# Late mask rows for the odd head, nine unread products and a buffer for expert 0's input, in a fused attention, router, expert and gated-layer kernel

## The chip, the cores and the metric

One core of one Trainium2 chip runs the whole program in one launch. The metric is device time in microseconds (us), the median of the runs shown; lower is better. In the profile PE is the matrix engine, PEld its weight loads, DVE the vector engine, ACT the scalar engine, POOL the GpSimd engine and SP the engine that issues most DMAs (SPq in a row is its queue).

## The reference

Three stages, each feeding the next. Attention has 2 batches of 8 heads, 768 positions and 64 columns; a query sees only the keys whose nearest centroid (of 16) is its own:

```python
q_assign = np.argmax(np.einsum('bhsd,hcd->bhsc', q_n, c_n), axis=-1)
k_assign = np.argmax(np.einsum('bhsd,hcd->bhsc', k_n, c_n), axis=-1)
mask = q_assign[:, :, :, None] == k_assign[:, :, None, :]
scores = np.where(mask, scale * np.matmul(q, k.transpose(0, 1, 3, 2)), -1000000000.0)
...
return np.matmul(attn, v).astype(np.float32)
```

A router then sends each of the 1536 rows to one of 8 experts by the largest of 8 logits (at most 384 rows each); an expert computes `relu(x @ w1) @ w2` with 512 x 1024 and 1024 x 512 weights, scaled by the gate. A gated layer with 512 x 1536 weights ends it: `(silu(x @ w_gate) * (x @ w_val)) @ w_out`.

## The kernel before

Numbers are kept as a rounded high part and a low part of the rest (H and L, or W1h and W1l), and products are added from three pairings, so that single-pass matmuls give nearly full precision.

**Attention.** Two heads of a batch make a pair; there are 8 pairs. The loop of `Attention.run` (L568) goes over 96 row tiles g of 128 query rows, 12 to a pair: g=0 to 5 are pair 0's even head and g=6 to 11 its odd head (`group`, L338; in the last pair, from g=84 on, the two heads change every three tiles). Scores of a tile come from two products into one PSUM tile (`qk`, L363): `Aq` x `Ak` and `qB` x `kB`. The mask is part of the second product: 16 rows of `qB` and `kB` hold the one-hot cluster of a query, and of a key scaled and shifted by 2**100, so that unequal clusters get a huge negative score. For the even head these rows are 64 to 79 (80 rows are read); for the odd head they are 48 to 63 of the other half of the tile (all 128 rows are read). `soft` takes the exponential, `pt` transposes it in two halves through two PSUM buffers in turn (T0 is copied out by ACT, T1 by DVE), `pv` multiplies with v once per three tiles, `evac` (L419) takes that out.

Within one tile the steps go by `CFG['order']` (S, E, Q, T0, T1, B0, O, V0, B1): S is `soft(g + 1)`, Q is `qk(g + 2)`, E the evacuation at every third tile, B0 the first of the background steps that `bg[g]` holds, and B1 the rest. `CFG['offs1']` says at which tile each preparation step of pair 1 stands (`k0`, `k1` transposes, `a`, `t`, `f` the cluster assignment, `m0`, `m1` its mask), `CFG['offs']` that of the later pairs.

Pair 0 is prepared ahead of the loop. `mask0` (L278) transposes the one-hots, writes the even head's mask rows straight from PSUM (L294, L297), and then copies everything to `oT` (L305, L306), from where two DMAs put the odd head's rows in place (L308 to L310). `unit` (L110) then clears `R`, loads the gate weights into it by six small DMAs and copies identities; `early` sets up the router on POOL; `low` makes pair 1's low part, and `moves` (L200) issues DMAs for pair 1's q. In tile 0 `load(2, "qk")` loads pair 2's q and k by four DMAs. SP issues DMAs strictly in the order in which the program gives them.

**Weights of expert 0.** They come in eight blocks of 512 KB (`load`, L952), through four rotating buffers `raw`. From tile 81 (`g0`, L1519) on they are split into a high and a low part while attention still runs: `piece(i, k, eng)` (L977) converts half k of block i, the high part on ACT (eng 1) or POOL (eng 0), the low part on POOL. The table at L1523 to L1527 says where each half stands; those of the list `pieces` run at the evacuations of tiles 85, 88 and 91, one ahead of `evac` and one behind it. When the second half of a block is done its buffer can be taken by a later load. `slots` (L1000) names the tile `XA`, expert 0's first 128 input rows, without writing it; the first write is in `take_head` (L1008). `tail` (L1072) does expert 0's first products while the router ends; block 7 is converted there whole.

```python
    def slots(self):
        self.XA = self.raw.tile([128, 2, self.KD, 128], F32R, tag="raw", name="XA")
```

Of the kernel before, what the change touches and what calls it, by code (L numbers as in the profile page):

```python
# [10 lines left out]
F32 = mybir.dt.float32  # L11
# [12 lines left out]
class Attention:  # L24
# [137 lines left out]
    def tr(self, n, nm, half):  # L162
# [10 lines left out]
        nc.scalar.activation(out=Ht[:, sl], in_=flat, func=AF.Copy, scale=s)  # L173
        if CFG["xe"]["qk".index(nm)] == "a":
            nc.scalar.activation(out=X[:, sl], in_=flat, func=AF.Copy, scale=s)
# [102 lines left out]
    def mask0(self):  # L278

        nc, st = self.nc, self.pairs[0]  # L280
        J, C, S = self.J, self.C, self.S
        HJ = J // 2
        st["oT"] = self.one.tile([4 * C, S], F32R, tag="oT", name="oT")
        ohv = st["oh"].rearrange("p j s c -> p j (s c)")
        ps = []
        for half in range(2):
            t = self.ps_m.tile([4 * C, HJ, 128], F32, tag="mm", name="otp")
            for jj in range(HJ):
                nc.tensor.transpose(t[:, jj, :], ohv[:, half * HJ + jj, :], self.ident)
            ps.append((slice(half * HJ * 128, (half + 1) * HJ * 128), t.rearrange("p j t -> p (j t)")))  # L290
        q, k = slice(0, 2 * C), slice(2 * C, 4 * C)

        def queries(sl, flat):
            nc.vector.tensor_copy(st["Bq"][64:64 + C, 0, sl], flat[0:C])  # L294

        def keys(sl, flat):
            nc.scalar.activation(out=st["Bk"][64:64 + C, 0, sl], in_=flat[2 * C:3 * C], func=AF.Identity,  # L297
                                 scale=self.sc[2 * C:3 * C, 0:1], bias=self.sc[2 * C:3 * C, 1:2])

        keys(*ps[0])  # L300
        queries(*ps[1])
        keys(*ps[1])
        queries(*ps[0])
        for sl, flat in ps:
            nc.vector.tensor_copy(st["oT"][q, sl], flat[q])  # L305
            nc.scalar.activation(out=st["oT"][k, sl], in_=flat[k], func=AF.Identity, scale=self.sc[k, 0:1],  # L306
                                 bias=self.sc[k, 1:2])
        for si, nm in enumerate("qk"):  # L308
            r0 = 2 * si * C
            self.move(st["B" + nm][64 - C:64, 1], st["oT"][r0 + C:r0 + 2 * C])  # L310

    def mask(self, n, half):
        nc, st = self.nc, self.pairs[n]
# [189 lines left out]
    def run(self, cent, gate, early, fill, after, spare, pieces, go):  # L503
# [5 lines left out]
        bg = {}  # L509
        for n in range(1, self.NP):  # L510
            s0 = 2 * J * (n - 1)
            st = self.prep_steps(n)
            for nm, o in CFG["offs" if n > 1 else "offs1"]:
                if n == 1 and nm in ("q0", "q1"):
                    continue
                bg.setdefault(s0 + o, []).append(st[nm])
            if n + 1 < self.NP:
                bg.setdefault(s0 + CFG["load"], []).append(lambda n=n: self.load(n + 1, "qk"))
            if n > 1:
# [13 lines left out]
        a = [self.assign0(0), self.assign0(1)]  # L533
# [1 line left out]
            next(a[i])  # L535
        low = self.tr0(1, "q")
        self.warm(self.ps_m, "mm", 18)
        self.mask0()
        self.unit(gate)
        early()  # L540
        self.unit2()
        low()
        self.moves(1, 0, "q")
        self.moves(1, 1, "q")
        for e in range(self.E + 1):
            bg.setdefault(14 + 4 * e, []).append(lambda e=e: fill(e))
        for g, st in spare.items():
# [1 line left out]
        self.qk(0)  # L549
        self.soft(0)  # L550
        self.qk(1)

        chains, moves, ready = [], [], {}
        outs = {}
        for G in range(4 * self.NP - 1):
            n, half, r = self.group(G)
            if r == 1:
                outs[(G + 1) * HJ + CFG["oc"][half if n + 1 < self.NP else 2]] = n, half

        def trickle(g, tok):  # L560
            if chains and tok in CFG["mt" if g < NG - 2 * J else "mt2"] and g >= chains[0][0]:
                if next(chains[0][1]) is None:
                    moves.append(chains.pop(0)[1])
            if moves and tok == CFG["pt"] and g not in (s0 + 7, s0 + 8):
                if next(moves[0], 0) == 0:
# [73 lines left out]
            pass  # L639


CFG = {'px': 'a', 'mt2': ['S', 'E', 'Q', 'T0'], 'mt': ['B1'], 'pt': 'V0', 'pe': 1, 'ms': [5, 2, 2], 'mr': 5, 'order': ['S', 'E', 'Q', 'T0', 'T1', 'B0', 'O', 'V0', 'B1'], 'offs': [['k0', -3], ['q0', -2], ['q1', -1], ['k1', 0], ['a', 1], ['t', 3], ['f', 6], ['m0', 7], ['m1', 8]], 'xe': 'da', 'me': 'a', 'ee': 'a', 'ec': 1, 'oc': [5, 5, 2], 'offs1': [['q0', 4], ['k0', 0], ['k1', 1], ['a', 2], ['t', 3], ['f', 5], ['m0', 6], ['m1', 7], ['q1', 0]], 'load': 0}


class Router:
# [251 lines left out]
class Experts:  # L897
# [101 lines left out]

    def slots(self):  # L1000
        self.XA = self.raw.tile([128, 2, self.KD, 128], F32R, tag="raw", name="XA")

    def turn_head(self, at):
        self.pa = at.ps_m.tile([128, self.KD, 128], F32, tag="mm", name="xa")
# [67 lines left out]
    def tail(self, at, go):  # L1072

        nc, rt, KD = self.nc, self.rt, self.KD
        self.room(at)
        a = self.fold(0)
        off = rt.offsets(self.keep[1], at.ps_t.tile([128, 3, 128], F32, tag="t", name="t")[:, 0, 0:self.E])
        next(a)
        yield
        self.rows(0, 0, 1, 2)  # L1080
        nc.gpsimd.memset(rt.gap, 0.0)
        next(a)
        next(a)
        go(4)
        for _ in range(6):
            next(off)
        next(a)
        for i in off:
            end = i
        go(12)  # L1090
        a = self.fold(1)
        rt.after(self.split(0, 7), [end])
        for _ in a:
            pass
        b = self.head2(at)
        for _ in range(16):
            next(b)
        self.cnt0, self.cnt1 = [self.count(1, e, None, rt.CP) for e in range(2)]
        for _ in range(8):
            next(b)  # L1100
        self.px = [at.ps_s.tile([128, 2, 512], F32, tag="s", name="xp") for _ in range(2)]
        for k in range(KD):
            self.turn(0, k)
        with self.tc.If(self.cnt0 > 128):
            for k in range(KD):
                self.turn(1, k)
            with self.tc.If(self.cnt0 > MERGED):
                for k in range(KD):
                    self.turn(2, k)
        for _ in b:  # L1110
            pass
# [374 lines left out]
def tile_clustered_attention_moe_swiglu(ctx, tc, q, k, v, cent, gate, w1, w2, wg, wv, wo, out, cap):  # L1486
    nc = tc.nc
    B, H, S, D = q.shape
    J = S // 128
    E, DM, F = w1.shape  # L1490
# [3 lines left out]
    with tc.manual_schedule():  # L1494
        ident = const.tile([128, 128], F32, name="ident")
        with ExitStack() as c2:
# [3 lines left out]
            with ExitStack() as c1:  # L1500
# [4 lines left out]
                ex = Experts(tc, rt, w1, w2, ident, raw, keep)  # L1505
# [7 lines left out]
                def first():  # L1513
# [5 lines left out]
                g0 = 2 * J * (at.NP - 2) + 9  # L1519
                at.free = g0 + 4  # L1520
                P = lambda i, h, eng: lambda: ex.piece(i, h, eng)
                L = lambda i: lambda: ex.load(i)
                pieces = [P(1, 1, 1), P(2, 0, 1), P(3, 1, 1), P(4, 0, 1), P(5, 1, 1), P(6, 0, 1)]  # L1523
                spare = {g0: [first], g0 + 1: [L(1), P(0, 0, 0)], g0 + 2: [L(2), P(0, 1, 0)], g0 + 3: [L(3), P(1, 0, 0)],
                         g0 + 5: [P(2, 1, 0)], g0 + 6: [P(3, 0, 0)], g0 + 8: [P(4, 1, 0)],
                          g0 + 9: [at.most, P(5, 0, 0), L(7)], g0 + 10: [lambda: None, lambda: ex.turn_head(at)],
                         g0 + 11: [ex.take_head, P(6, 1, 0)]}  # L1527
                go = lambda n, it=ex.head1(at): [next(it) for _ in range(n)]
                front = at.run(cent, gate, rt.setup, rt.fill, after, spare, pieces, go)
                next(front)  # L1530
# [42 lines left out]
```

## Time and profile before

| | |
|---|---|
| median of 3 runs | 757.07 us (756.25 to 758.7) |
| profiled execution | 760.44 us; its span (first to last instruction) 758.7 us |
| busy share of the span | PE 97%, PEld 81%, DVE 68%, ACT 52%, POOL 37% |
| PE clock granted, mean | 0.989 of full |
| DMA | 102.92 MB, 136 GB/s on average |

The profiled execution is 3.4 us above the median; lengths of stalls are read from it, and a change of time is then put on the median. The clock is given as a share of 2.4 GHz: 0.50 in a row is the level of 1.2 GHz. A row of the order of time reads: start, length, engine, line, operation, output and inputs, how often; in square brackets how long the engine had been idle before it and what ended that.

### The profile page before, as it was taken

What the parts mean: (1) busy time and instruction counts of PE and PEld (TensorE: products, weight loads), DVE (VectorE), ACT (ScalarE), POOL (GpSimd) and SP (SyncE); (2) the same over time, 40 slices, a digit from 0 to 9 for tenths busy, and PEclk for the clock granted to TensorE, in tenths of its full rate; (3) what the DMA queues carried; (4) which work ended last, traced back from release to release, by engine and by line L of the source; (5) the groups of instructions that cost most, each with busy time, mean ns of one, the idle gap of its engine ahead of it and who ended that gap; (6) DMA issues with size and microseconds to landing.
All of it is one profiled execution on the core that took longest, in us unless ns stands there. A gap on an engine that the chain in (4) does not pass through costs nothing.

```text
span 758.7 us, 12766 instructions
## 1 busy us (share of the span) xinstructions
PE 736.1 (97%) x4334; PEld 614.3 (81%) x4334; DVE 512.7 (68%) x864; ACT 394.5 (52%) x762; POOL 280.0 (37%) x267
## 2 busy tenths in 40 slices
PE   7999999999999999999989999999999999999996
PEld 6777777777776799899989998788888888888885
DVE  4677778788786857666775657776676667677333
ACT  6677686777778655567756543453223322322210
POOL 6120220212216754445772433442333332333245
PEclk9999999999999999999989999999999999999999
DMA  9758869548256345888876642331212211210012
GB/s 207 173 134 201 208 181 251 130 93 188 51 135 205 98 152 185 264 252 272 261 242 196 199 142 83 84 112 58 81 56 73 67 57 55 69 42 1 1 56 111
DMA packets 103790, 102.92 MB, mean 136 GB/s; under 512 B 30896, under 2 KB 90800, under 8 KB 103696
## 3 DMA queue, kind: packets, MB, share of 16 engines
q1 hardware_dynamic: 101632, 95.37, 45.4%
q0 software_dynamic: 1920, 6.29, 2.2%
q8 instruction: 56, 0.92, 0.5%
q14 instruction: 38, 0.31, 0.1%
q10 hardware_dynamic: 144, 0.03, 0.0%
HBM read 68.48 MB, written 12.85 MB: 107 GB/s over the span
## 4 chain that ended last, share of the span: by engine, by line
PE 46%; DVE 4%; issue 4%; ACT 3%; DMA 3%; POOL 2%; ACTq 0%; POOLq 0%; DVEq 0%; SPq 0%
PE o L1439 12%; PE g L1421 12%; PE v L1421 11%; DMA raw<-in_moe_w 3%; PE yp L1207 3%; PE hp L1207 2%; PE yp L1199 2%; PE hp L1199 2%; PE yp L1208 1%; POOL rhot L885 1%; PE hp L1208 1%; DVE gtmp L1398 1%; ACT W1h L968 1%; POOL out L1450 1%; DVE gtmp L1397 0%
## 5 line engine op out<-in xcount | busy, mean ns | idle before, releaser
L368 DVE TENSOR_REDUCE nm<-s 128x1 f32<-128x768 f32 x96 | 91.1, 950 | 12.8 <-PE s L365 11.3
L969 POOL TENSOR_TENSOR W2l<-raw,W2h 128x1024 fp32r<-128x1024 f32 x29 | 68.9, 2392 | 74.6 <-ACT W2h L968 74.5
L378 ACT ACTIVATE P<-s,nm 128x768 f32<-128x768 f32 x96 | 86.5, 901 | 12.4 <-DVE nm L368 12.1
L397 PE MATMUL t<-ident,P 128*128 128x128 f32 x576 | 81.1, 275 | 1.1 <-ACT PT L400 0.9
L1428 POOL TENSOR_TENSOR ghl<-u,ghh 128x512 fp32r<-128x512 f32 x36 | 50.1, 1391 | 76.1 <-ACT ghh L1427 76.1
L397 PEld LDWEIGHTS t<-ident,P 128*128 128x128 f32 x576 | 68.8, 141 | 7.7 <-DVE PT L402 2.0
L416 PE MATMUL acc<-PT,ldv 128*64 128x384 f32 x384 | 69.2, 494 | 0.0
L1207 PE MATMUL yp<-H,W2h 128*128 128x256 f32 (+3 forms) x224 | 65.2, 370 | 3.7 <-DVE H L1228 3.7
L1447 DVE TENSOR_TENSOR acc<-o,acc 128x512 f32<-128x512 f32 x60 | 41.5, 691 | 33.1 <-PE o L1439 32.9
L365 PE MATMUL s<-Ak,Aq 128*128 128x384 f32 x192 | 58.7, 387 | 4.8 <-ACT P L378 3.9
L1425 DVE TENSOR_TENSOR u<-sg,g 128x512 f32<-128x512 f32 x36 | 24.7, 687 | 54.4 <-ACT sg L1424 54.4
L1207 PE MATMUL hp<-X,W1h 128*128 128x256 f32 (+3 forms) x224 | 60.8, 352 | 0.3 <-ACT W2h L968 0.3
L400 ACT COPY PT<-t 128x384 f32<-128x384 f32 x96 | 45.7, 476 | 27.9 <-PE t L397 27.7
L1427 ACT CAST ghh<-u 128x512 fp32r<-128x512 f32 x36 | 22.4, 622 | 68.2 <-DVE u L1426 68.2
L1208 PE MATMUL yp<-H,W2l 128*128 128x128 f32 (+3 forms) x224 | 55.8, 249 | 0.0
L1208 PE MATMUL hp<-X,W1l 128*128 128x128 f32 (+3 forms) x224 | 54.0, 241 | 0.0
L402 DVE COPY PT<-t 128x384 f32<-128x384 f32 x96 | 52.4, 546 | 1.1 <-PE t L397 1.1
L365 PEld LDWEIGHTS s<-Ak,Aq 128*128 128x128 f32 x192 | 29.2, 190 | 29.1 <-ACT P L378 18.1
L365 PE MATMUL s<-kB,qB 80*128 80x384 f32 (+1 forms) x192 | 50.3, 343 | 0.5 <-DVE oT L305 0.3
L969 DVE TENSOR_TENSOR W1l<-raw,W1h 128x1024 fp32r<-128x1024 f32 x28 | 41.5, 1499 | 12.0 <-ACT W1h L968 11.7
L1207 PEld LDWEIGHTS yp<-H,W2h 128*128 128x128 f32 x224 | 44.6, 199 | 4.5 <-issue 3.9
L416 PEld LDWEIGHTS acc<-PT,ldv 128*64 128x64 f32 x384 | 25.1, 136 | 28.0 <-issue 27.2
(301 smaller groups left out, 1915.4 us busy)
## 6 DMA issues: line engine op xcount, KB each, us to landing
raw<-in_moe_w SPq DMA_DIRECT2D x64, 512.0 KB, 4.9
Ak<-Hk SPq DMA_DIRECT2D x32, 192.0 KB, 4.2
moe_rows<-zero SPq DMA_DIRECT2D x8, 768.0 KB, 5.1
xr<-moe_rows SPq DMA_DIRECT2D x24, 256.0 KB, 4.9
raw<-in_moe_w_gate SPq DMA_DIRECT2D x12, 512.0 KB, 3.6
raw<-in_moe_w_val SPq DMA_DIRECT2D x12, 512.0 KB, 3.6
raw<-in_moe_w_out SPq DMA_DIRECT2D x12, 512.0 KB, 3.6
ldq<-in_q SPq DMA_DIRECT2D x16, 192.0 KB, 4.4
```

Of the source, the lines that this page charges most:

```text
L365: nc.tensor.matmul(ps[:, c, 0:HS], lhsT=ql[:, qs], rhs=kr[:, c * HS:(c + 1) * HS], start=a == 0, stop=a == 1)
L368: nc.vector.tensor_reduce(out=nm, in_=ps[:, :, 0:HS], axis=AX.XY, op=ALU.max, negate=True)
L378: nc.scalar.activation(out=P, in_=ps[:, :, 0:HS], func=AF.Exp, bias=nm, accum_out=self.pairs[n]["sum"][:, i, r:r + 1])
L397: nc.tensor.transpose(ps[:, jj, :], P[:, a, jj * 128:(jj + 1) * 128], self.ident)
L402: nc.vector.tensor_copy(PT[:, js, cs], ps)
L416: nc.tensor.matmul(acc[c * D:(c + 1) * D], lhsT=v[:, c * HJ + j], rhs=PT[:, c * HJ + j, :], start=j == 0, stop=j == HJ - 1, tile_position= ...
L969: j = (nc.vector if e and i < 4 else nc.gpsimd).tensor_tensor(out=l, in0=t, in1=h.bitcast(F32), op=ALU.subtract)
L1207: self.nc.tensor.matmul(out[:, :, 0:w], lhsT=W[0][:, k, cols], rhs=mov[:, :, k, 0:w], start=k == 0, stop=False)
L1208: self.nc.tensor.matmul(out[:, 0, 0:w], lhsT=W[1][:, k, cols], rhs=mov[:, 0, k, 0:w], start=False, stop=k == ks - 1)
L1421: nc.tensor.matmul(ps[which], lhsT=W[a], rhs=self.Y[b][:, k, ts], start=k + i == 0, stop=k == KD - 1 and i == 2)
L1428: nc.gpsimd.tensor_tensor(out=hl[:, fc], in0=u, in1=hh[:, fc].bitcast(F32), op=ALU.subtract)
L1439: nc.tensor.matmul(p[t], lhsT=h[a][:, fc, t * 128:(t + 1) * 128], rhs=W[b][:, fc], start=fc == 0 and i == 0, stop=fc == 1 and i == 2)
```

## The change

1. `mask0` becomes a generator in three parts. Ahead of the loop only the transposes and the even head's rows run; the first half of the copies to `oT` runs as the first background step of tile 0, the second half and the two DMAs as the first of tile 1.
2. `unit(gate)` runs after `low` instead of before `early`.
3. Nine transposes of the identity, which nobody reads, are issued to PE behind `qk(1)`, ahead of tile 0 (and so ahead of `qk(2)`).
4. Pair 1's steps `k0` to `m1` stand one tile later.
5. `slots` clears two elements of `XA`, so that the tile takes its buffer there and then.
6. Block 6 of expert 0's weights: its first half is done on POOL in tile 92, its second on ACT in `tail`; before, the first was on ACT in tile 91 and the second on POOL in tile 92.

```diff
--- before.py
+++ after.py
@@ -301,13 +301,17 @@
         queries(*ps[1])
         keys(*ps[1])
         queries(*ps[0])
+        yield
         for sl, flat in ps:
             nc.vector.tensor_copy(st["oT"][q, sl], flat[q])
             nc.scalar.activation(out=st["oT"][k, sl], in_=flat[k], func=AF.Identity, scale=self.sc[k, 0:1],
                                  bias=self.sc[k, 1:2])
+            if sl.start == 0:
+                yield
         for si, nm in enumerate("qk"):
             r0 = 2 * si * C
             self.move(st["B" + nm][64 - C:64, 1], st["oT"][r0 + C:r0 + 2 * C])
+        yield
 
     def mask(self, n, half):
         nc, st = self.nc, self.pairs[n]
@@ -535,13 +539,16 @@
             next(a[i])
         low = self.tr0(1, "q")
         self.warm(self.ps_m, "mm", 18)
-        self.mask0()
-        self.unit(gate)
+        masks = self.mask0()
+        next(masks)
         early()
         self.unit2()
         low()
+        self.unit(gate)
         self.moves(1, 0, "q")
         self.moves(1, 1, "q")
+        for g in range(2):
+            bg.setdefault(g, []).insert(0, lambda: next(masks))
         for e in range(self.E + 1):
             bg.setdefault(14 + 4 * e, []).append(lambda e=e: fill(e))
         for g, st in spare.items():
@@ -549,6 +556,7 @@
         self.qk(0)
         self.soft(0)
         self.qk(1)
+        self.warm(self.ps_t, "t", 9)
 
         chains, moves, ready = [], [], {}
         outs = {}
@@ -639,7 +647,7 @@
             pass
 
 
-CFG = {'px': 'a', 'mt2': ['S', 'E', 'Q', 'T0'], 'mt': ['B1'], 'pt': 'V0', 'pe': 1, 'ms': [5, 2, 2], 'mr': 5, 'order': ['S', 'E', 'Q', 'T0', 'T1', 'B0', 'O', 'V0', 'B1'], 'offs': [['k0', -3], ['q0', -2], ['q1', -1], ['k1', 0], ['a', 1], ['t', 3], ['f', 6], ['m0', 7], ['m1', 8]], 'xe': 'da', 'me': 'a', 'ee': 'a', 'ec': 1, 'oc': [5, 5, 2], 'offs1': [['q0', 4], ['k0', 0], ['k1', 1], ['a', 2], ['t', 3], ['f', 5], ['m0', 6], ['m1', 7], ['q1', 0]], 'load': 0}
+CFG = {'px': 'a', 'mt2': ['S', 'E', 'Q', 'T0'], 'mt': ['B1'], 'pt': 'V0', 'pe': 1, 'ms': [5, 2, 2], 'mr': 5, 'order': ['S', 'E', 'Q', 'T0', 'T1', 'B0', 'O', 'V0', 'B1'], 'offs': [['k0', -3], ['q0', -2], ['q1', -1], ['k1', 0], ['a', 1], ['t', 3], ['f', 6], ['m0', 7], ['m1', 8]], 'xe': 'da', 'me': 'a', 'ee': 'a', 'ec': 1, 'oc': [5, 5, 2], 'offs1': [['q0', 4], ['k0', 1], ['k1', 2], ['a', 3], ['t', 4], ['f', 6], ['m0', 7], ['m1', 8], ['q1', 0]], 'load': 0}
 
 
 class Router:
@@ -999,6 +1007,7 @@
 
     def slots(self):
         self.XA = self.raw.tile([128, 2, self.KD, 128], F32R, tag="raw", name="XA")
+        self.nc.gpsimd.memset(self.XA[0:1, 0, 0, 0:2].bitcast(F32), 0.0)
 
     def turn_head(self, at):
         self.pa = at.ps_m.tile([128, self.KD, 128], F32, tag="mm", name="xa")
@@ -1089,6 +1098,7 @@
             end = i
         go(12)
         a = self.fold(1)
+        self.piece(6, 1, 1)
         rt.after(self.split(0, 7), [end])
         for _ in a:
             pass
@@ -1520,11 +1530,11 @@
                 at.free = g0 + 4
                 P = lambda i, h, eng: lambda: ex.piece(i, h, eng)
                 L = lambda i: lambda: ex.load(i)
-                pieces = [P(1, 1, 1), P(2, 0, 1), P(3, 1, 1), P(4, 0, 1), P(5, 1, 1), P(6, 0, 1)]
+                pieces = [P(1, 1, 1), P(2, 0, 1), P(3, 1, 1), P(4, 0, 1), P(5, 1, 1)]
                 spare = {g0: [first], g0 + 1: [L(1), P(0, 0, 0)], g0 + 2: [L(2), P(0, 1, 0)], g0 + 3: [L(3), P(1, 0, 0)],
                          g0 + 5: [P(2, 1, 0)], g0 + 6: [P(3, 0, 0)], g0 + 8: [P(4, 1, 0)],
                           g0 + 9: [at.most, P(5, 0, 0), L(7)], g0 + 10: [lambda: None, lambda: ex.turn_head(at)],
-                         g0 + 11: [ex.take_head, P(6, 1, 0)]}
+                         g0 + 11: [ex.take_head, P(6, 0, 0)]}
                 go = lambda n, it=ex.head1(at): [next(it) for _ in range(n)]
                 front = at.run(cent, gate, rt.setup, rt.fill, after, spare, pieces, go)
                 next(front)
```

Three places show what moves. On **SP**, at the start of the program (before, ahead of the gate loads; `R` is the gate matrix, `qB_111` and `kB_113` are pair 0's tiles, `_112` and `_114` pair 1's):

```order
L138 DMA ldv<-in_v 128x384 x2
L150 DMA qB_111<-oT 16x768
L150 DMA kB_113<-oT 16x768
L117 DMA R<-in_moe_w_gate 64x4x8
L119 DMA R_116<-in_moe_w_gate 64x8 x2
```

The odd head's two DMAs stood ahead of the six gate loads, which pair 1's six q moves and pair 2's four loads follow. Now on **SP**, behind those sixteen (one piece of the difference):

```order
 L138 DMA ldq<-in_q 128x6x64 x2
 L138 DMA ldk<-in_k 128x6x64 x2
+L150 DMA qB_111<-oT 16x768
+L150 DMA kB_113<-oT 16x768
 L150 DMA Ak<-Hk 64x768 x2
 L150 DMA kB_114<-Lk 64x768
```

The two DMAs moved behind the last load of pair 2's k, ahead of pair 1's k moves. The second place is **SP** from tile 82 on, the loads of expert 0's blocks 2, 4, 3, the input rows, and blocks 5, 6, 7, with what each waits for. Each of eight semaphores (DMAHW0 to 7) belongs to every eighth DMA in turn, so a wait on another DMA's semaphore tells whose buffer is taken. Before:

```order
L960 DMA raw_3057<-in_moe_w1 128x4x256 [waits DMAHW0_49]
L960 DMA raw_3064<-in_moe_w2 128x4x256 [waits DMAHW1_49]
L960 DMA raw_3092<-in_moe_w1 128x4x256 [waits DMAHW6_49,DMAHW2_49,Pool_49]
L994 DMA raw_3113<-moe_rows 128x512 [waits DMASW4_49,DMASW3_49,DMASW5_49,DMASW2_49,DMAHW3_49,DMASW1_49,DMAHW7_49,DMASW0_49,Pool_49]
L960 DMA raw_3195<-in_moe_w2 128x4x256 [waits DMAHW0_49,DMAHW4_49,Activation_49,Pool_49]
L960 DMA raw_3240<-in_moe_w2 128x4x256 [waits DMAHW5_49,DMAHW2_49,Pool_49]
L960 DMA raw_3279<-in_moe_w2 128x4x256 [waits DMAHW1_49,Activation_49,Pool_49]
```

Block 5 (`raw_3195`, own semaphore 4) took the buffer of block 2 (semaphore 0), block 6 that of block 3 (semaphore 2), block 7 that of block 4 (semaphore 1). And now:

```order
L968 DMA raw_3067<-in_moe_w1 128x4x256 [waits DMAHW0_49]
L968 DMA raw_3074<-in_moe_w2 128x4x256 [waits DMAHW1_49]
L968 DMA raw_3102<-in_moe_w1 128x4x256 [waits DMAHW6_49,DMAHW2_49,Pool_49]
L1002 DMA raw_3123<-moe_rows 128x512 [waits DMASW4_49,DMASW3_49,DMASW5_49,DMASW2_49,DMAHW3_49,DMASW1_49,DMAHW7_49,DMASW0_49,Pool_49]
L968 DMA raw_3206<-in_moe_w2 128x4x256 [waits DMAHW4_49,DMAHW2_49,Pool_49]
L968 DMA raw_3251<-in_moe_w2 128x4x256 [waits DMAHW1_49,DMAHW5_49,Activation_49,Pool_49]
L968 DMA raw_3290<-in_moe_w2 128x4x256 [waits DMAHW4_49,Pool_49]
```

`XA` holds block 2's buffer, so block 5 takes that of block 3, block 6 that of block 4 and block 7 that of block 5: each waits for the block one further on. The third place is **ACT** at tile 91, from the exponential of tile 92 to that of tile 93 (`ol` and `PT` are the evacuation and the T0 copy of tile 91). Before:

```order
L378 ACTIVATE P,sum<-s,nm 128x768
L983 CAST W2h<-raw 128x2x256
L431 COPY ol<-acc 64x384
L983 CAST W2h<-raw 128x2x256
L400 COPY PT<-t 128x3x128
L378 ACTIVATE P,sum<-s,nm 128x768
```

The cast ahead of `ol` is block 5's second half, the one behind it block 6's first. And now:

```order
L382 ACTIVATE P,sum<-s,nm 128x768
L991 CAST W2h<-raw 128x2x256
L435 COPY ol<-acc 64x384
L404 COPY PT<-t 128x3x128
L382 ACTIVATE P,sum<-s,nm 128x768
```

Only block 5's cast is left there, ahead of `ol`.

## Rows read from the trace of the kernel before

**Rows 1.** Busy time by engine in stretches; us, then PE, PEld, DVE, ACT, POOL, clock, DMA.

```profile
31.00:46.00 15.00, 14.37 (x92) 10.16 (x90) 10.07 (x17) 11.44 (x24) 1.00 (x1) 1.00 0.79 175
100.00:200.00 100.00, 98.81 (x668) 73.33 (x667) 77.04 (x148) 73.92 (x162) 15.94 (x16) 1.00 0.61 145
```

**Rows 2.** PE in order of time, 10 to 31 us.

```profile
10.73 2.13 PE L501 MATMUL warm<-ident 128*128 128x128 f32 x18
...
15.70 0.59 PE L365 MATMUL s<-kB,qB 80*128 80x384 f32 x2 [0.25 <-DVE oT L305]
...
18.36 1.01 PE L365 MATMUL s<-Ak,Aq 128*128 128x384 f32 x2 [1.36 <-ACT P L378]
...
27.43 0.49 PE L231 MATMUL ast<-ident,as 128*128 128x128 f32 x3
...
30.39 0.52 PE L365 MATMUL s<-kB,qB 128*128 128x384 f32 x2
```

**Rows 3.** ACT, DVE and PE in order of time, tiles 91 and 92.

```profile
252.03 0.61 ACT L983 CAST W2h<-raw 128x512 fp32r<-128x512 f32 x1
252.89 0.48 ACT L431 COPY ol<-acc 64x384 f32<-64x384 f32 x1 [0.26 <-PE acc L416]
255.21 0.62 ACT L983 CAST W2h<-raw 128x512 fp32r<-128x512 f32 x1 [1.84 <-DMA raw<-in_moe_w]
...
253.40 0.55 DVE L433 TENSOR_TENSOR O<-acc,ol 64x384 f32<-64x384 f32 x1 [1.30 <-ACT ol L431]
253.98 0.96 DVE L368 TENSOR_REDUCE nm<-s 128x1 f32<-128x768 f32 x1
254.86 0.55 DVE L402 COPY PT<-t 128x384 f32<-128x384 f32 x1
...
256.38 0.87 PE L397 MATMUL t<-ident,P 128*128 128x128 f32 x6 [0.91 <-ACT PT L400]
```

**Rows 4.** SP's queue in order of time, 21 to 34 us.

```profile
21.10 0.57 SPq L150 DMA_DIRECT2D qB<-oT  x1
...
22.40 0.68 SPq L117 DMA_DIRECT2D R<-in_moe_w_gate  x1
...
26.38 0.59 SPq L150 DMA_DIRECT2D Aq<-Hq  x1
...
33.62 0.65 SPq L138 DMA_DIRECT2D ldk<-in_k  x1
```

**Rows 5.** DMA issues at 21.77 us and 33.62 us: KB each, us from issue to landing.

```profile
kB<-oT SPq DMA_DIRECT2D x1, 48.0 KB, 2.3
...
ldk<-in_k SPq DMA_DIRECT2D x1, 192.0 KB, 4.4
```

**Rows 6.** Busy time in stretches, as rows 1: the clock behind two waits of PE.

```profile
18.00:19.00 1.00, 0.64 (x2) 0.64 (x3) 0.15 (x1) 1.00 (x4) 0.00 (x0) 0.55 1.05 222
...
21.00:22.00 1.00, 1.00 (x8) 1.00 (x7) 0.56 (x2) 0.34 (x2) 0.00 (x0) 0.74 0.77 206
...
400.00:401.00 1.00, 1.00 (x7) 1.00 (x7) 0.00 (x0) 0.31 (x1) 0.00 (x0) 0.80 0.95 331
```

**Rows 7.** PE behind its longest wait in the experts, in order of time.

```profile
395.03 0.66 PE L1207 MATMUL yp<-H,W2h 128*128 128x384 f32 x1 [3.36 <-DVE H L1228]
```

**Rows 8.** POOL at 22.8 us; ACT, POOL and PE at 275 to 278 us.

```profile
22.78 1.00 POOL L176 TENSOR_TENSOR Lk<-Xk,Hk 128x384 fp32r<-128x384 f32 x1 [6.47 <-ACT Xk L175]
...
275.39 0.59 ACT L1054 COPY hA<-ha 128x512 f32<-128x512 f32 x1 [0.62 <-PE ha L1024]
...
276.04 2.38 POOL L969 TENSOR_TENSOR W2l<-raw,W2h 128x1024 fp32r<-128x1024 f32 x1
...
277.46 0.33 PE L1023 MATMUL ya<-HA,W2h 128*128 128x256 f32 x1
```

**Rows 9.** SP's issue of block 6 of expert 0, and its landing.

```profile
251.57 0.37 SPq L960 DMA_DIRECT2D raw<-in_moe_w  x1
...
raw<-in_moe_w SPq DMA_DIRECT2D x1, 512.0 KB, 3.6
```

## The prediction

> **What bounds the kernel now.** I read the busy time by stretch first. Between 100 and 200 us PE is busy for 98.81 of 100 us, and between 31 and 46 us for 14.37 of 15 [rows 1]: once attention runs, PE has under 5% to give, so a wait put into its stream near the start is not earned back, and removing another engine's work there earns nothing unless PE had waited for it. The order of time of PE then shows where it does wait: 1.36 us ahead of tile 2's scores, for the first exponential [rows 2], and 0.91 us in tile 92, for a copy by ACT [rows 3]. Those two the change touches. Last I read SP's queue, since the change reorders it: between 21.10 and 34.27 us it issues one DMA behind the other with no pause [rows 4]. It is full just where two DMAs are put back in it.
>
> **The change, part by part.**
>
> *The odd head's rows.* The two `oT` DMAs stood at 21.10 us; from there to the first gate load at 22.40 is 1.30 us for both. The sixteen DMAs that are now ahead of them (six gate loads, six moves, four loads) fill 22.40 to 33.62 + 0.65 = 34.27, that is 11.87 us [rows 4]. They now start at 21.10, so the two are issued at about 33.0 and 33.65. The data they carry is ready long before, so SP's place decides, not the new steps in tiles 0 and 1. Landing has two bounds. Alone, such a DMA took 2.3 us: 33.65 + 2.3 = 35.95. Behind the last k load it can't be much ahead of that one's data: this was issued at 33.62 and took 4.4 us [rows 5], so 38.02, now 1.30 earlier, 36.72, plus up to 0.65 for the second issue, 37.4. I take 37.0, nearer the second bound, since the queue is the same. Tile 6, the odd head's first, needs those rows; its second product began at 30.39 [rows 2]. PE takes its work in order, so everything behind stands too: 37.05 - 30.39 = **6.7 us** (5.6 to 7.1).
>
> *Pair 1's steps one tile later.* Three transposes, 0.49 us at 27.43 [rows 2], stood ahead of that product and now come behind the wait: **+0.5**. The rest of the shift moves PE work among tiles that PE fills anyway; later pairs already have their last mask step at that place, in the stretch with 98.81% [rows 1], so I cost it at nothing.
>
> *The clock.* Ahead of 18.4 us PE waits 1.36 us, and the granted clock falls to 0.50, is 0.55 on average in 18 to 19 us and rises in the middle of 21 to 22 [rows 2, 6]: 18.36 to 21.5 is 3.15 us at 1.2 GHz, half of it, 1.6, lost. Behind the wait of 3.36 us PE starts at 395.03 and the clock rises at about 400.4 (0.80 in that us): 5.4 us low, 2.7 lost [rows 6, 7]. The new wait is about 8 us long, so the clock will be low behind it: 1.6 to 2.7, I take **+2.1**. What the other engines have ready after it lets PE close some of the 0.63 us that it idled in 31 to 46 us [rows 1]: **-0.4**.
>
> *Nine unread products, copies out of the way.* Nine cost 9/18 of 2.13 us, 1.07 [rows 2], and stand in the 1.36 us wait ahead of tile 2. They should keep the clock up there (1.6 us), and PE's 0.25 us wait for the first `oT` copy goes [rows 2]. Both come ahead of tile 6, so they only make the wait longer: **0**. The copies, now in tiles 0 and 1, end there too, as do the nine products if their cover were gone (at most 1.07).
>
> *`unit` behind `low`.* POOL idles 6.47 us up to 22.78 [rows 8], which hides it; the gate loads aren't due before 21.10. **0**.
>
> *`XA`'s own buffer and block 6.* The element clear takes a buffer, so block 5's load now waits for block 3's conversion, the event at which block 6's load was issued before, at 251.57, landing 3.6 us later [rows 9]; with 0.1 us for the clear on POOL, 255.3. But block 5's cast still stands ahead of `ol` on ACT, at 252.03 [rows 3], and everything on ACT stands behind it. Before, ACT had waited 1.84 us for block 6 there, up to 255.21, behind `ol`. Now the wait is 3.2 us, with `ol` behind it. After it: cast to 255.95, `ol` to 256.4, T0 copy to 256.85, and on DVE, which waits for `ol`, the sum (0.55), the maximum (0.96) and the T1 copy (0.55), one behind the other, with hand-overs to 258.5; before, the T1 copy ended at 255.41 [rows 3]. PE's second half of tile 92's transposes needs that buffer: it stood at about 256.8 and now comes at 258.55: **+1.8 us**, instead of the 0.9 that leaving out block 6's cast would give were block 5 there in time. Bounds: -0.9 and, if the two waits of PE that this makes (about 1.2 us each) drop the clock as the one of 1.36 did, 1.8 + 1.6 = 3.4.
>
> *The second half of block 6 in the tail.* On ACT its 0.62 us fits the 0.62 that ACT idles ahead of 275.39. On POOL its low part (half of 2.38, about 1.25) runs first from 276.04, to 277.3; the first product to read it is that at 277.46 [rows 8]. **0**, with 0.2 to spare; if the cover is gone, a few tenths.
>
> **Sum**: 6.7 + 0.5 + 2.1 - 0.4 + 1.8 = 10.7 us. The profiled execution, 760.44 us around a span of 758.7, would be 771.1. The median of the runs, 3.4 us lower, 757.07, becomes **767.8**.
>
> A rule that speaks about the first term: the Trainium skill, "DMA: Bandwidth & Descriptors", section "Issuing engines are not separate DMA queues", says that the time a sequencer takes to start a DMA is usually small beside the DMA itself. Were it so here, the gate loads, which carry a few KB each, would not hold SP, and the third rival below would come. The trace disagrees: they hold SP for 22.40 to 26.38, 3.98 us for six [rows 4].
>
> **The rivals.**
>
> 1. *The rows land in time, and it is faster.* If SP's pace were not tied to the number of DMAs and the odd head's rows were there when PE reaches tile 6, the wait wouldn't exist. PE would reach it at 30.39 - 0.25 - 1.6 = 28.5; that is the point that decides, 8.5 us ahead of my landing. What is left is the gain of the start, 1.85, and with block 5 in time 0.9 more: 757.07 - 2.75 = 754.3. For it: the changed pieces are all aimed at waits that the trace shows. Against: sixteen issues in 5 us would be 0.3 us each; the rows show 0.57 to 0.68. Chance 0.08.
> 2. *Only the first wait comes.* Block 5 lands sooner, or its wait is hidden, and the 0.9 of tile 92 is gained: 10.7 - 1.8 - 0.9 = 8.0, 765.1. For it: tile 92's chain is short, and I built it from durations that may overlap. Chance 0.17.
> 3. *A shorter first wait.* The issue of the gate loads hides behind the data still moving at 21 us, and the two DMAs come 3.98 us sooner: landing at 33.0, a wait of 2.7 instead of 6.7: 763.8. Against: SP's rows there follow one another without a pause. Chance 0.09.
> 4. *No change*: gains of the start and losses of tile 92 cancel with the rows in time: 757.07 - 1.85 + 1.8 = 757.0. Chance 0.03.
>
> **How the numbers follow.** My forecast, both waits, has 0.63. Its own range is 764.5 (first term 5.6, clock 1.6, tile 92 at no loss) to 771 (7.1, 2.7 and 3.4 in their place). With rivals 2 and 3, which lie at 765.1 and 763.8 with 1 us of spread in the runs (756.25 to 758.7), I take 762.5 to 771.5; it leaves out rivals 1 and 4 and tails of the rest. A measurement of this kernel can tell about 0.3%, 2.3 us, from no change. Slower by more: 0.63 + 0.17 + 0.09 = 0.89; faster by more, rival 1: 0.08; within: 0.03.
>
> **What the changed profile would show.** Right: SP issues the two `oT` DMAs at 33 to 34 us; tile 6's 128-row product starts at 36.5 to 37.5 us behind an idle PE of 7 us or more that a DMA of `oT` ends; the clock is 0.50 until some 3 to 5 us after it; a clock near 1.00 at 18 to 21 us, ahead of it; block 5's cast on ACT idle for about 3 us, and two PE waits in tile 92. From tile 7 to tile 90 the same lengths as before, later by some 9 us. Wrong: the 128-row product at 29 us, with no DMA wait; then the SP argument is false and the result lies near 754 to 757. If the first wait is there but PE's stretch of tile 92 is not longer than before, the step on `XA`'s buffer is false.

## The result, and the profile after

| | before | after |
|---|---|---|
| median, measured together | 756.66 us (755.86 to 758.7, 4 runs) | 767.93 us (766.57 to 769.84, 4 runs) |
| ratio, 95% interval | | 1.0145 [1.0126, 1.0165] |
| profiled execution; its span | | 767.62 us; 765.9 us |
| PE clock granted, mean | | 0.991 |

The change made the kernel slower by 11.3 us (9.5 to 12.5 by the interval). Against [rows 4], SP's queue in order of time:

```profile
21.03 0.66 SPq L117 DMA_DIRECT2D R<-in_moe_w_gate  x1
...
23.69 1.25 SPq L119 DMA_DIRECT2D R<-in_moe_w_gate  x2
...
29.35 2.06 SPq L138 DMA_DIRECT2D ldq<-in_q  x2
31.52 1.29 SPq L138 DMA_DIRECT2D ldk<-in_k  x2
32.91 0.80 SPq L150 DMA_DIRECT2D qB<-oT  x1
33.81 0.55 SPq L150 DMA_DIRECT2D kB<-oT  x1
```

The landing of the second one (KB each, us from issue to landing), against 2.3 in [rows 5]:

```profile
kB<-oT SPq DMA_DIRECT2D x1, 48.0 KB, 4.2
```

PE in order of time, against [rows 2]:

```profile
15.61 0.59 PE L369 MATMUL s<-kB,qB 80*128 80x384 f32 x2 [0.37 <-DMA kB<-Lk]
...
16.74 1.15 PE L505 MATMUL warm<-ident 128*128 128x128 f32 x9
18.28 0.62 PE L369 MATMUL s<-Ak,Aq 128*128 128x384 f32 x2 [0.39 <-ACT P L382]
...
21.91 0.55 PE L169 MATMUL trp<-ident,ldk 128*128 128x128 f32 x3 [0.60 <-ACT oT L307]
22.93 0.62 PE L369 MATMUL s<-Ak,Aq 128*128 128x384 f32 x2 [0.47 <-ACT P L382]
...
25.91 0.62 PE L369 MATMUL s<-Ak,Aq 128*128 128x384 f32 x2 [1.01 <-ACT P L382]
...
30.34 0.62 PE L369 MATMUL s<-Ak,Aq 128*128 128x384 f32 x2
38.25 0.98 PE L369 MATMUL s<-kB,qB 128*128 128x384 f32 x2 [7.30 <-DMA kB<-oT]
...
41.59 0.84 PE L369 MATMUL s<-kB,qB 128*128 128x384 f32 x2
...
43.55 0.52 PE L369 MATMUL s<-kB,qB 128*128 128x384 f32 x2
```

The wait of 7.30 us stands where it was expected. The nine products do shorten the wait ahead of tile 2 (0.39 instead of 1.36), yet tile 6 is reached no sooner: three new waits, for the copies to `oT` on ACT and for the exponentials queued behind them, take the gain.

Busy time in stretches (the clock is the third column from the right), against [rows 1, 6]:

```profile
18.00:21.00 3.00, 2.72 (x19) 2.59 (x20) 1.78 (x4) 1.59 (x5) 0.00 (x0) 1.00 0.95 208
36.00:43.00 7.00, 4.75 (x20) 4.59 (x21) 3.17 (x5) 1.41 (x3) 0.59 (x1) 0.51 0.71 160
268.00:272.00 4.00, 4.00 (x19) 3.79 (x19) 2.54 (x4) 2.35 (x7) 1.85 (x3) 0.57 0.44 131
100.00:200.00 100.00, 99.09 (x670) 73.55 (x668) 78.44 (x150) 72.29 (x159) 16.08 (x16) 1.00 0.71 169
```

The clock is up at 18 us, low behind the long wait, and low a second time at 268 us. In the middle nothing changed: 99.09 beside 98.81 of 100 us. Tiles 91 and 92 on ACT and PE, against [rows 3]:

```profile
264.66 0.62 ACT L991 CAST W2h<-raw 128x512 fp32r<-128x512 f32 x1 [3.02 <-DMA raw<-in_moe_w]
265.30 0.48 ACT L435 COPY ol<-acc 64x384 f32<-64x384 f32 x1
...
266.33 0.55 PE L401 MATMUL t<-ident,P 128*128 128x128 f32 x3 [1.34 <-ACT PT L404]
267.87 0.67 PE L401 MATMUL t<-ident,P 128*128 128x128 f32 x3 [0.99 <-DVE PT L406]
```

Block 5's cast waits 3.02 us with `ol` behind it, and PE waits twice; the low clock follows. Expert 0, on DVE and POOL, against [rows 8]:

```profile
288.08 0.15 DVE L838 TENSOR_TENSOR offi<-eps,zero 128x1 int32<-128x1 f32 x1
288.15 1.96 DVE L839 TENSOR_TENSOR offi<-rkd,zero 128x7 int32<-128x7 f32 x1
...
288.79 1.29 POOL L992 TENSOR_TENSOR W2l<-raw,W2h 128x512 fp32r<-128x512 f32 x1
```

An operation on seven numbers per partition shows 1.96 us and ends with POOL's, that is with block 6's second half, which the change puts there. That I had not expected.

For the experiments I cut each execution at five points: PE's first `kB` x `qB` product, tile 6's, pair 1's first, the start of expert 0's first products, and the start of the last of its second ones. "In place" below means read between these points.

| profiled execution | first product | to tile 6 | to pair 1 | to expert 0 | its two products |
|---|---|---|---|---|---|
| before | 15.70 | 14.69 | 15.07 | 221.0 | 16.6 |
| after | 15.61 | 22.64 | 16.58 | 224.1 | 17.6 |

The differences are 7.95, 1.51, 3.1 and 1.0 us, 13.6 together, more than the 11.3 of the medians; the last section says why.

### The profile page after: what moved, and what is told of

Same layout as the page of the kernel before. It is cut to its first block, busy times and chain, and to the rows that moved or that the text cites. A ratio compares the mean times of both kernels' runs of the same rounds, so it can differ in the third digit from the quotient of the medians.

```text
span 765.9 us, 12786 instructions
## 1 busy us (share of the span) xinstructions
PE 736.7 (96%) x4343; PEld 613.9 (80%) x4343; DVE 509.7 (67%) x864; ACT 394.8 (52%) x762; POOL 280.7 (37%) x268
## 4 chain that ended last, share of the span: by engine, by line
PE 54%; DVE 3%; ACT 1%; POOL 1%; DMA 1%; issue 1%; ACTq 0%; POOLq 0%; DVEq 0%
PE o L1449 12%; PE g L1431 11%; PE v L1431 11%; PE yp L1217 5%; PE hp L1217 5%; PE yp L1218 2%; PE hp L1218 2%; PE yp L1209 2%; PE hp L1209 2%; DVE gtmp L1408 1%; PE xp L1173 1%; POOL out L1460 1%; DMA xr<-moe_rows 1%; DVE gtmp L1407 0%; DVE gtmp L1409 0%
## 5 line engine op out<-in xcount | busy, mean ns | idle before, releaser
L372 DVE TENSOR_REDUCE nm<-s 128x1 f32<-128x768 f32 x96 | 91.2, 951 | 22.8 <-PE s L369 18.4
L1217 PE MATMUL yp<-H,W2h 128*128 128x256 f32 (+3 forms) x224 | 61.6, 354 | 0.6 <-DVE H L1238 0.2
L1218 PE MATMUL yp<-H,W2l 128*128 128x128 f32 (+3 forms) x224 | 54.2, 242 | 0.1
L977 DVE TENSOR_TENSOR W1l<-raw,W1h 128x1024 fp32r<-128x1024 f32 x28 | 42.3, 1525 | 14.1 <-ACT W1h L976 13.6
L176 POOL TENSOR_TENSOR Lk<-Xk,Hk 128x384 fp32r<-128x384 f32 x14 | 14.0, 1001 | 89.0 <-ACT Xk L175 89.0
```

Source lines behind the costliest of these rows:

```text
L372: nc.vector.tensor_reduce(out=nm, in_=ps[:, :, 0:HS], axis=AX.XY, op=ALU.max, negate=True)
L977: j = (nc.vector if e and i < 4 else nc.gpsimd).tensor_tensor(out=l, in0=t, in1=h.bitcast(F32), op=ALU.subtract)
L1217: self.nc.tensor.matmul(out[:, :, 0:w], lhsT=W[0][:, k, cols], rhs=mov[:, :, k, 0:w], start=k == 0, stop=False)
L1218: self.nc.tensor.matmul(out[:, 0, 0:w], lhsT=W[1][:, k, cols], rhs=mov[:, 0, k, 0:w], start=False, stop=k == ks - 1)
```

## The experiments

My theory had two waits: SP's queue delays the odd head's rows, and `XA`'s buffer delays block 5. The rivals: a cost that lies in the clock or in the copies, or in block 6's new places. Each kernel was timed beside the kernel before in one session (medians of before 756.81, 756.91 and 755.89 in three sessions: runs 1 to 4, 5 to 8 on another chip, 9 to 12), so I compare ratios, not times, across sessions.

**1. The change, with pair 1's moves and pair 2's loads behind the two DMAs.**

```diff
-            if n + 1 < self.NP:
+            if 1 < n and n + 1 < self.NP:
...
-        self.moves(1, 0, "q")
-        self.moves(1, 1, "q")
...
+        for f in (lambda: self.moves(1, 0, "q"), lambda: self.moves(1, 1, "q"), lambda: self.load(2, "qk")):
+            bg[1].append(f)
```

> The changed kernel with one edit: pair 1's six q moves and pair 2's four loads are issued behind the two oT DMAs instead of ahead of them; the copies stay in tiles 0 and 1, the gate loads stay in front. Theory (SP's place of the two DMAs makes the wait): they are issued at about 25 to 26 us, land by about 28.5, tile 6's 128-row product starts at about 31 us instead of 38.25, no low clock behind it, so 7.3 + 2.3 = 9.6 us less than 767.9: about 758.3. Rival (the copies in tiles 0 and 1 come too late for the odd head, whatever SP does): tile 6 still waits and the time stays at 766 to 769.

Measured: 759.17 us, ratio 1.0046 [1.0016, 1.0076]; 15.18 us to tile 6. SP, then PE:

```profile
25.50 0.57 SPq L150 DMA_DIRECT2D qB<-oT  x1
26.16 0.53 SPq L150 DMA_DIRECT2D kB<-oT  x1
```

```profile
30.43 0.62 PE L369 MATMUL s<-Ak,Aq 128*128 128x384 f32 x2
30.88 0.52 PE L369 MATMUL s<-kB,qB 128*128 128x384 f32 x2
```

No wait is left, and 1.0145 falls to 1.0046: some 7.5 us of the 11 hang on the place of two DMAs in SP's queue.

**2. The change without the clear of `XA`.**

```diff
-        self.nc.gpsimd.memset(self.XA[0:1, 0, 0, 0:2].bitcast(F32), 0.0)
```

> The changed kernel without the clear of two elements of XA. Theory (the clear takes the buffer that block 5's load had, so that ACT waits for block 5 ahead of the evacuation of tile 91): block 5's load is issued one block earlier, ACT's cast of it does not wait, and tile 91 to 93 shorten by the 2.35 us lost against before and the 0.9 us that before lost: 767.9 - 3.3 = 764.6, or 763 if a low clock goes with it. Rival (the move of block 6's halves makes the wait): no change, 767 to 769.

Measured: 765.22 us, ratio 1.0108 [1.0087, 1.013]; 220.8 us to expert 0. ACT and PE in tile 93:

```profile
267.96 0.59 ACT L1019 CAST XA<-xa 128x512 fp32r<-128x512 f32 x1 [1.54 <-POOL W2l L992]
```

```profile
269.33 2.16 PE L420 MATMUL acc<-PT,ldv 128*64 128x384 f32 x12 [1.06 <-DVE XA L1020]
```

The clear costs 3.3 us in place and 2.8 in the ratio (0.0037 of 757). Without it tile 92's wait of 0.91 [rows 3] is gone, but `XA` waits for a buffer and PE 1.06 us one tile later: block 6's move gains nothing there.

**3. Before, with only the mask rows late** (`mask0` with the `yield`s of the change, `unit` behind `low`).

```diff
...
-        self.mask0()
-        self.unit(gate)
+        masks = self.mask0()
+        next(masks)
...
+        self.unit(gate)
...
+        for g in range(2):
+            bg.setdefault(g, []).insert(0, lambda: next(masks))
```

> The kernel before with the late mask rows and the later gate set-up alone (no unread products, pair 1's steps, clear and block 6 as before). Theory: the first wait alone accounts for most of the change: tile 6's product at about 38, low clock behind it: 756.7 + 9 = 765 to 766.5. Rival (the loss is shared out over the parts, or the nine products cost it): under 761.

Measured: 764.71 us, ratio 1.01 [1.0078, 1.0121]. This part alone makes two thirds of the loss. Its profiled execution started late, and PE waited for a copy to `oT` on the way to tile 6:

```profile
26.16 0.55 PE L169 MATMUL trp<-ident,ldk 128*128 128x128 f32 x3 [2.01 <-ACT oT L307]
...
38.85 0.59 PE L369 MATMUL s<-kB,qB 128*128 128x384 f32 x2 [2.10 <-DMA kB<-oT]
```

The first product came at 19.77 us (15.61 in the change), the wait for the copy took 2.01 us and the clock fell behind it (0.50 in 28 to 30 us), so the wait for the rows is 2.10 instead of 7.30: the rows come by SP's time, not by PE's.

**4 and 12. The change, with the wait filled by 56 unread transposes** (run twice, the second time beside the change itself, run 11).

```diff
+                if tok == "Q" and g == 4:
+                    self.warm(self.ps_t, "t", 56)
```

> The changed kernel with 56 more unread 128x128 transposes ahead of tile 6's products, which fill about 6.7 us of the 7.3 us that PE idles there. Theory (the low clock behind the wait costs half of its 4.6 us): the product still starts at about 38.3, the clock stays at 1.00 behind it, 2.3 us less: 765.6. Rival (the low clock is hidden, since other engines set the pace behind the wait): no change, 767.9, or slower if the products push the tile out.

> The change itself, on the same chip as the kernel that fills the wait. 767.9 as before; tile 6's 128-row product to pair 1's first product 16.6 us with a low clock behind the wait.

> The change with 56 unread transposes ahead of tile 6's products, beside the change itself on one chip. Theory: the clock term is real and stays to the end, tile 6 to pair 1 15.1 us instead of 16.6, and the median 1.5 to 2 us below that of the change, 766. Rival: what the clock gives is taken back later, by waits for later pairs' mask rows, and the two medians agree within 0.5 us: then the low clock behind the wait cost only place, not time.

Measured: 769.6 us, ratio 1.0168 [1.0143, 1.0193], the first time; the second time 767.32, ratio 1.0152 [1.013, 1.0175], beside 768.45, ratio 1.017 [1.0148, 1.0192], for the change. The clock stayed at 1.00, and tile 6 to pair 1 took 15.12 and 15.06 us, beside 16.58 and 16.50 in the change: the low clock costs 1.45 us there. The medians don't show it, once above the change and once below. In run 4, with an early start (16.30) and tile 6 at 38.20, it was taken back later: PE waited 0.62 us at 115.6 us, for which the profile names no cause, and again for a later pair's mask rows:

```profile
210.01 0.59 PE L369 MATMUL s<-kB,qB 80*128 80x384 f32 x2 [0.97 <-DMA qB<-oT]
```

Neither wait stands in the change, and expert 0 began at 279.06 us, beside 278.96 in the change. In run 12 no such wait stands, but the start was late (19.94), and PE's order of time shows another loss:

```profile
34.76 6.34 PE L505 MATMUL warm<-ident 128*128 128x128 f32 x56
40.85 0.59 PE L369 MATMUL s<-Ak,Aq 128*128 128x384 f32 x2
41.28 0.52 PE L369 MATMUL s<-kB,qB 128*128 128x384 f32 x2
```

No wait is left behind the fill, since the rows had landed at 38.8 (issued at 35.00, 3.8 us): the fill itself held PE some 2 us too long. A fixed fill fits only one start. So in one execution the 1.45 us were gone before expert 0, as the rival of run 12 has it, in the other they can't be told, and whether they last in general is not settled.

**5. Before, with the nine products and both halves of block 6 on POOL in tile 92.**

```diff
+        self.warm(self.ps_t, "t", 9)
...
-                pieces = [P(1, 1, 1), P(2, 0, 1), P(3, 1, 1), P(4, 0, 1), P(5, 1, 1), P(6, 0, 1)]
+                pieces = [P(1, 1, 1), P(2, 0, 1), P(3, 1, 1), P(4, 0, 1), P(5, 1, 1)]
...
-                         g0 + 11: [ex.take_head, P(6, 1, 0)]}
+                         g0 + 11: [ex.take_head, P(6, 0, 0), P(6, 1, 0)]}
```

> Kernel before plus the nine unread products ahead of tile 0, and both halves of block 6 on POOL in tile 92 (none on ACT, none in the tail). My theory: the start keeps its clock at 1.00 (gain up to 1.6 us in that place, less what new waits of tiles 0 to 5 take) and tile 92 loses PE's wait of 0.91 us, so 1.5 + 0.9 below before: about 754.3 against 756.7, pair 1's first product (45.5 us before) earlier by 1.5. Rival: the start is set by ACT and DVE, not by PE's clock, so PE waits for the exponential again and tile 6 is reached no earlier than 30.3; then only tile 92's 0.9 is left, 755.8, or nothing, 756.7.

Measured: 755.47 us, ratio 0.9983 [0.996, 1.0005], not told apart from before. First product at 16.73, 13.23 us to tile 6 (14.69 before, 14.82 in run 7, which has no nine products either): the start gains 1.5. Tile 92's wait again moves to `XA`:

```profile
258.70 2.16 PE L416 MATMUL acc<-PT,ldv 128*64 128x384 f32 x12 [0.88 <-DVE XA L1013]
```

**6. Before, with the nine products alone** (the first line of the diff of 5).

> Kernel before plus the nine unread products alone. My theory: the granted clock stays 1.00 from 18 to 21.5 us and tile 6's first 128-row product comes at 28.9 instead of 30.4 us (before, without the copies to oT in tiles 0 and 1 that the change puts there): 755.2 against 756.7. Rival (ACT and DVE set the pace of tiles 2 to 5): the clock stays up but the product still comes at 30.3, with new waits of PE for P and oT of 0.5 to 1 us each, and the time is 756.7.

Measured: 756.84 us, ratio 0.9984 [0.996, 1.0007]. The execution started late: 19.99, and 13.50 us to tile 6. Run 8, which has no nine products, also started late (20.00) and took 13.48, with the clock at 1.00 from 18 us on although PE waited:

```profile
22.93 0.61 PE L365 MATMUL s<-Ak,Aq 128*128 128x384 f32 x2 [1.55 <-ACT P L378]
```

So the nine products save 1.5 us where the start is early and nothing where it is late; the medians can't show that. What makes a start late can be read too. The 18 unread products ahead of the loop, 2.13 us at 10.73 in [rows 2], took nearly twice that in run 6:

```profile
14.25 3.98 PE L501 MATMUL warm<-ident 128*128 128x128 f32 x18
```

The granted clock was 0.50 there, from 8 to 17 us. In the six traces with a first product by 16.3 us or, in run 5, at 16.73, these products took 2.13 us, in run 2 (16.62) 2.67, in the seven with one at 18.07 to 20.01 us 3.50 to 4.05: PE prepares pair 0 at the low clock. (In runs 3, 8 and 12 the lengths alone show it; the column of the clock reads 1.00 there.) Why the clock is low there in some executions is not shown.

**7. Before, with block 6 moved as in the change, without the clear.**

```diff
+        self.piece(6, 1, 1)
...
-                pieces = [P(1, 1, 1), P(2, 0, 1), P(3, 1, 1), P(4, 0, 1), P(5, 1, 1), P(6, 0, 1)]
+                pieces = [P(1, 1, 1), P(2, 0, 1), P(3, 1, 1), P(4, 0, 1), P(5, 1, 1)]
...
-                         g0 + 11: [ex.take_head, P(6, 1, 0)]}
+                         g0 + 11: [ex.take_head, P(6, 0, 0)]}
```

> Kernel before plus the move of block 6 alone (first half on POOL in tile 92, second on ACT in the tail), XA without a buffer of its own until it is written. My theory: PE's wait of 0.91 us in tile 92 goes (pair 1's first product to expert 0's first product 0.9 us shorter than the 221.0 of before), and the tail gives it back: POOL's low part of block 6 holds up the small DVE operations and PE waits about 0.7 us in expert 0's second products, which take 8.8 us instead of 8.0. Sum 0: 756.7. Rival: the tail's longer products come from another part of the change, so they stay at 8.0 and the time is 755.8.

Measured: 756.81 us, ratio 1.0002 [0.9979, 1.0025]; 220.8 us to expert 0, not 0.9 less (PE waited 1.06 us for `XA`); its second products took 8.8 us, against 8.1 in runs 5, 6 and 8. DVE, then POOL:

```profile
275.61 1.98 DVE L829 TENSOR_TENSOR offi<-roff,zero 128x7 int32<-128x7 f32 x1
277.52 0.15 DVE L830 TENSOR_TENSOR offi<-eps,zero 128x1 int32<-128x1 f32 x1
```

```profile
276.26 1.30 POOL L984 TENSOR_TENSOR W2l<-raw,W2h 128x512 fp32r<-128x512 f32 x1
```

The tail's loss belongs to block 6's second half. The expectation had the gain in tile 92 and was wrong there.

**8. Before, with the clear of `XA` alone.**

```diff
+        self.nc.gpsimd.memset(self.XA[0:1, 0, 0, 0:2].bitcast(F32), 0.0)
```

> Kernel before plus the clear of two elements of XA alone, block 6 as before. My theory: block 5's load waits for block 3's conversion and block 6's for block 4's, so ACT waits for both in tiles 91 and 92, ahead of ol and behind it: pair 1's first product to expert 0's first product 2 to 4 us longer than the 221.0 of before, with a low clock behind it, 759 to 760.7. Rival: as in the change it is only 3 us, because block 6's load was the last anyway: 758.5 or less; or the clear costs nothing and the late stretch came from block 6: 756.7.

Measured: 761.17 us, ratio 1.0059 [1.0033, 1.0085]; 225.6 us to expert 0, 4.6 more than before. ACT, then PE:

```profile
258.31 0.62 ACT L983 CAST W2h<-raw 128x512 fp32r<-128x512 f32 x1 [3.06 <-DMA raw<-in_moe_w]
258.95 0.47 ACT L431 COPY ol<-acc 64x384 f32<-64x384 f32 x1
261.61 0.62 ACT L983 CAST W2h<-raw 128x512 fp32r<-128x512 f32 x1 [2.19 <-DMA raw<-in_moe_w]
```

```profile
262.79 0.87 PE L397 MATMUL t<-ident,P 128*128 128x128 f32 x6 [4.19 <-ACT PT L400]
```

Both blocks are late, each load waiting for a conversion one block further on. Block 6's move takes the second of these waits off ACT: together (3.1) the two edits cost less than the clear alone.

**9. The change, with only pair 2's loads behind the two DMAs.**

```diff
+        bg[1].append(lambda: self.load(2, "qk"))
```

(The loop that appends `load(n + 1)` skips n = 1, as in run 1.)

> The change with only pair 2's four loads put behind the odd head's two DMAs (the six gate loads and pair 1's six moves stay ahead of them). My theory (SP's place sets the wait, about 0.6 to 0.65 us for each DMA ahead): the two are issued at 29.3 and 29.9 us instead of 32.9 and 33.8, with a start like that of the change (first product at 15.6), and land 2.3 us later if they travel alone, 32.2, so that tile 6's 128-row product comes 16.6 us behind the first product (22.6 in the change, 15.2 with all ten moves and loads put behind). Were the landing as slow as in the change, 4.4 us, it would be 18.7. Total 761.5 to 764. Rival: the wait comes from the big loads' data, not from the issue, and goes wholly with the loads: 15.2 and 759.2 as with the rows ahead of everything.

Measured: 762.72 us, ratio 1.008 [1.0059, 1.0101], between run 1 and the change. SP, then PE; the first product came at 18.42:

```profile
29.91 0.94 SPq L150 DMA_DIRECT2D qB<-oT  x1
30.95 0.86 SPq L150 DMA_DIRECT2D kB<-oT  x1
```

```profile
34.12 0.59 PE L369 MATMUL s<-kB,qB 128*128 128x384 f32 x2 [0.27 <-DMA kB<-oT]
```

The two were issued 0.6 and 1.0 us later than expected, but 4.4 and 4.8 behind those of run 1, as the six moves hold SP for 4.2 us (25.04 to 29.26 in the change), and the rows land within 3.1 us of the second issue. So the moves do delay the rows, which the rival left out. In this later start little of that reaches PE: 0.27 us of wait is left, 15.70 us to tile 6 instead of the 16.6 expected for an early one. The time leans the same way, the ratio being 0.0034 above run 1's, but the two intervals overlap: how the 0.0099 from run 1 to the change divides between the six moves and the four loads is not settled.

**10. Runs 1 and 2 together: both causes out.**

> The change with both costs taken out: the odd head's two DMAs ahead of pair 1's moves and pair 2's loads, and XA not cleared. The nine products, the copies in tiles 0 and 1, pair 1's steps one tile later and block 6's halves stay. My theory: 759.2 less the 2.7 that the clear cost, 756.5, no different from before: the nine products' gain is spent on the copies, and that of tile 92 on the wait for XA's buffer and on the tail. Rival: the two gains that the change aimed at remain, 1.85 and 0.9, and it is 754 to 755.

Measured: 758.06 us, ratio 1.0029 [1.0012, 1.0046]; 15.25 us to tile 6 from a start at 20.01, 220.8 to expert 0, and 17.6 for its products. Of the theory's 756.5 the mechanism holds, but 2.2 us (0.9 to 3.5) remain: the tail's 1.0, and at the start 1.8 in a late execution (15.25 beside 13.48 in run 8; 0.5 in an early one, 15.18 in run 1 beside 14.69 before), where the waits for `oT` and `P` in tiles 2 to 5 that the change shows stand again (0.60, 0.47 and 1.02 us), and in a late start nothing pays for them. The rival's 754 to 755 is out. No version here beats the kernel before by what can be told apart; run 5 comes nearest.

## Why the prediction was right

The median came to 767.93 us, 767.8 was predicted, and the forecast's mechanism, both waits, is the one that runs 1 and 2 take apart. That the two numbers agree to 0.1 us is luck, as the terms show, in their order:

- **Odd head's rows**, +6.7 (5.6 to 7.1). Issues were put at 33.0 and 33.65 and came at 32.91 and 33.81. The landing, put at 37.0, came about 38.0: with 4.2 us the small DMA behind the loads took as long as a load, above both bounds. In place the term was 7.95 for the profiled start. But tile 6's product came at 38.2 to 39.0 us in five of the executions with the late rows (after, 2, 3, 4, 11) whether the first product came at 15.6 or at 19.8, since SP's queue runs on its own time (the second DMA was issued at 33.73 to 34.92 in these five); in an execution that starts late the loss is smaller: with the first product at 18.07 (run 11) the wait was 5.52. Pair 1's first product shows the size: 54.83 us in the change against 45.46 before, both early, is 9.4, but 55.51 (run 11) against 48.57 (run 8, before with the clear alone), both late, is 6.9. The prediction had one start, that of the trace, and I take this to be why four differences of 13.6 us make 11.3 in the medians; how often a start is late is not on record. (The two profiled executions differ by 7.2 us only, because the one of before lost some 6 us in the experts, 170.6 us from expert 0's end to the gated layer against 163.9 to 166.8 in every other execution: the waits of [rows 7].)
- **Pair 1's steps and the clock**, +0.5 + 2.1 - 0.4. In place +1.5. The clock was low from 38.25 to 42.9 us, where the products fall from 0.84 to 0.52 us: 4.6 us, 2.3 lost at PE; the steps cost nothing: with the wait filled, tile 6 to pair 1 took 15.1 us, as before. No run shows the -0.4 by itself, and whether the clock's part lasts to the end is open (runs 4 and 12).
- **Nine products and copies**, 0. Right in the change, where the wait that follows swallows both. Alone, each has a size: -1.5 for the products in an early start (run 5), +1.8 to +2.0 for the copies and what is queued behind them (15.25 in run 10 beside 13.48 in run 8, both late; 15.18 in run 1 beside 13.23 in run 5). The prediction's figure of 28.5 us at tile 6 without the rows' wait was wrong: run 1 reached it at 30.88.
- **`XA` and block 6 in tile 92**, +1.8 (-0.9 to 3.4). In place +3.1, near the upper bound. The step that failed is the choice between the bounds: the two waits of PE, put at about 1.2 us each and measured at 1.34 and 0.99, did drop the clock. The lower bound was wrong too: without the clear 0.9 is not gained, for `XA` then waits in its place (runs 2, 5, 7).
- **Block 6's second half in the tail**, 0. In place +1.0. The step that failed took POOL's low part to run beside DVE at no cost; a DVE operation beside it took 1.96 us, and PE waited 0.7 us for what DVE did behind that.

So the sum of 10.7 was close to 11.3 partly by errors that cancel: in place the first term was 1.3 us too small and the late ones 2.3, pair 1's steps and the clock 0.7 too large, and the first is smaller in executions that start later than the trace read. The forecast's own range was added up loosely: its terms give 764.4 to 770.4, not 764.5 to 771. The first and fourth rivals fall with the wait of 7.30 us. The third falls with SP's rows, where the six gate loads take 23.69 + 1.25 - 21.03 = 3.91 us again; the second with the wait of 3.02 us on ACT.

## What to carry to other kernels

A DMA is as late as its place in its issuer's queue: count every issue that a moved one is put behind, at its measured price (here 0.54 to 1.03 us each; ten of them and a slower landing made 7.5 us), before asking when its data are ready. When a buffer is claimed earlier, follow the whole rotation: every later load then waits for another conversion, and an engine that waits at the head of its queue holds work that needs no load. A gain that is spent before a wait in the same stream isn't a gain, and a wait that is removed at one tile has to be looked for in the next.

## What was not expected of the hardware

- **DVE held by POOL.** A 128 x 7 sum took 0.16 us in the kernel before; one of 1.90 to 2.01 us stands in all nine traces with block 6's second half in the tail, beside POOL's difference of 1.3 us, and in none of the other five. The Trainium skill, "SBUF — State Buffer", section "Who interferes with whom", says that a DVE instruction with two inputs in SBUF contends with a GpSimd instruction that reads SBUF, and calls the ports that they share an exclusive lock. The trace agrees at the end: POOL's ends at 290.08, the next DVE operation starts at 290.04. At the start it doesn't settle who held whom: the row of DVE begins 0.64 us ahead of POOL's.
- **Two waits of about a microsecond lowered the clock** (1.34 and 0.99, then 0.57 on average in 268 to 272 us), where one of 1.06 us in tile 93 of run 2 did not; a wait of 1.55 us in run 8 at 22.9 us did not either, while the 1.36 of [rows 2] did. In run 8 the 18 unread products had taken 3.73 us, as at the low clock, shortly before; in [rows 2] 2.13.
- **The start varies by over 4 us** between executions: the first product came at 15.6 to 20.0 us in the traces, by the clock that PE has while it prepares pair 0 (experiment 6). It decides what an edit at the start is worth.
